# Attention, two MLPs and a gate on one core: the attention's small matmuls in two groups a pair

## The chip, the cores and the metric

The kernel runs on one core of one Trainium2 chip. Its time is the device time of one launch in microseconds, and the time before is the median of three runs. Five engines work beside each other, each with its own queue, which it takes in order: TensorE (PE, matmuls into the accumulator memory PSUM), VectorE (DVE), ScalarE (ACT), GpSimd (POOL) and SyncE (SP, which issues the DMAs). They wait for each other through semaphores.

## The reference

Four batches of 768 tokens go through three stages. All is in float32.

```python
# 1. gated linear attention, 8 heads of 48 channels
for t in range(S):
    state = alpha[:, :, t, :, None] * state + einsum('bhd,bhe->bhde', k[:, :, t], v[:, :, t])
    y[:, :, t] = einsum('bhd,bhde->bhe', q[:, :, t], state)
# 2. x = y as (batch, 768, 384): mixing over tokens by a product of rank 32, then an MLP
h = x.transpose(0, 2, 1) @ U @ V
u = x + h.transpose(0, 2, 1)
x = u + maximum(u @ w_ch1, 0) @ w_ch2          # 384 -> 1536 -> 384
# 3. spatial gating unit
h = maximum(x @ w_in, 0);  u, v = h[..., :512], h[..., 512:]
v_n = (v - mean(v)) / sqrt(var(v) + 1e-6)
out = (u * (einsum('ts,bsd->btd', w_spatial, v_n) + b_spatial[None, :, None])) @ w_out
```

## The kernel before

Two heads make a pair, so there are 4 batches of 4 pairs, numbered 0 to 15. A pair's 768 tokens are cut into 6 chunks of 128. `prepare` (L605) makes running products of alpha over each chunk, backwards (`bw`, a scan on VectorE, L613) and forwards (`fw`, L625), and GpSimd multiplies k by the one and q by the other (L603). Then TensorE has these pieces, all in plain float32, in which one matmul stands as two records in the trace:

- `flip` (L645): five transposes of k; ScalarE copies them out of PSUM (`kn`, L657).
- `scores` (L661): for half the chunks, 6 matmuls k by q. Each uses 64 of TensorE's 128 rows, and the two heads run side by side. VectorE multiplies the result with the causal mask (`mask`, L678: 2 operations for each half).
- `added` (L684): what every chunk adds to the state, 10 matmuls with 64 of 128 columns each, and 2 more that multiply a tile of zeros (`nothing`), so that a scan over the chunks finds zeros where the next row begins. `state` (L697) is that scan on VectorE and two copies by ScalarE.
- `inner` and `outer` (L710, L721): 12 and 10 matmuls, masked scores by v and state by q; each writes 48 columns, the two heads side by side. ScalarE copies the result out in four pieces (`take`, L738).
- For three pairs of a batch there is also the mixing over tokens (`Mix`, L754): two times three transposes (`ps_t`, L763) and a product of 6 matmuls (`ps_g`, L779). These, like `flip`, use the whole array.

The MLP of a batch runs over two blocks of 384 tokens and 12 groups of 128 hidden channels. A group is `up_group` (L313: 9 matmuls in three triples) and, two groups behind, `down_group` (L339: 9 matmuls in three triples, one for each of three accumulators). Its matmuls split float32 into a high and a low part (type fp32r), and have 384 columns. After `up_group` ScalarE makes `h` from the bank (L328), and VectorE makes the remainder `hl` from the same bank (`rest_of_h`, L309), which then is free.

PSUM has 8 banks: 3 for the accumulators (`acc`), 2 for `up_group` (`mm`), and 3 for all of the attention (`x`).

The attention of batch b + 1 is woven into the MLP of batch b. `attend` (L796) is a generator; every `yield` ends a step. `pull` (L1018) is called after nearly every MLP triple and takes the next step when it is due, in equal shares, about one step for every three calls. So the order on each engine is the order in which the program issues: what a step issues stands on every engine behind what the MLP has issued until then and ahead of what comes next. A pair has 8 steps: flip (and the mixing's first transposes); the bw scan of the next pair; scores of the first half (and the second transposes) with their masks; the fw scan; added, scores of the second half, state and masks; a step for moves alone; (the product and) outputs; and loading. Batch 0's attention is `first_batch` (L889) and runs ahead of all this. In the MLP of batch 0 the weights are also loaded and unpacked, piece by piece: ScalarE (L195, L505), VectorE (L196, L199, L207) and GpSimd (L202).

## Time and profile before

| | |
|---|---|
| three runs | 722.79, 723.46, 724.92 us; median 723.46 |
| span of the profiled execution, first to last instruction | 722.5 us |
| PE busy | 699.7 us (97%) |
| PEld (weight loads, beside the matmuls) | 665.8 us (92%) |
| DVE, ACT, POOL busy | 341.0, 267.1, 203.8 us (47%, 37%, 28%) |
| TensorE's mean granted clock | 0.990 of full speed |

The profiled execution's own time is shown as its span alone. By the timeline the MLP of batch 0 runs from about 51 to 139 us, those of batches 1, 2 and 3 take some 87 us each after that, and the gating stage takes the rest, from 400 us on. Attention of batches 1 to 3, which the change touches, lies between 60 and 320 us. A row of the timeline has the start, the time from the first to the last end of the merged instructions, the engine, the line and the shapes. TensorE's instructions overlap: how long one keeps the engine is read from the start of one row to the start of the next.

### The profile page before, as it was taken

To read this page: it belongs to the slowest core of one execution; us is meant where nothing else is said; L and a number is where in the kernel's file an instruction comes from. 1 tells how busy PE (TensorE), PEld (TensorE's weight loads), DVE (VectorE), ACT (ScalarE), POOL (GpSimd) and SP (SyncE) were. 2 spreads that over 40 slices of the span, in tenths; PEclk is the share of its full clock that TensorE was granted. 3 is DMA by queue.
4 is the path that set the end of the run, shared out by engine and by line. 5 is a ranking of instruction groups with operands and counts; after the bars stand their busy time and mean duration, and the time that the engine had idled before them with its cause. 6 is when DMAs were issued, how large, how long until landed. Compare 5 with 4: busy or idle time off the path is not lost.

```text
span 722.5 us, 12138 instructions
## 1 busy us (share of the span) xinstructions
PE 699.7 (97%) x4984; PEld 665.8 (92%) x4984; DVE 341.0 (47%) x585; ACT 267.1 (37%) x542; POOL 203.8 (28%) x171
## 2 busy tenths in 40 slices
PE   7988699999999999999999999999999999999996
PEld 6877599999999999999999999989989989999996
DVE  8877879846444434443332486253152134226211
ACT  3874266643444332444331444232232223224111
POOL 4445434414110122010030043334224123433211
PEclk9999899999999999999999999999999999999998
DMA  9699043330532230500001545120003003000001
GB/s 343 205 341 222 1 80 70 67 68 34 109 73 48 61 59 1 111 5 2 34 1 37 189 131 169 48 73 1 34 1 99 33 1 99 1 33 2 33 34 38
DMA packets 21170, 54.01 MB, mean 75 GB/s; under 512 B 2705, under 2 KB 12817, under 8 KB 19825
## 3 DMA queue, kind: packets, MB, share of 16 engines
q1 hardware_dynamic: 21104, 53.14, 26.6%
q8 instruction: 41, 0.67, 0.4%
q14 instruction: 25, 0.20, 0.1%
HBM read 42.51 MB, written 9.44 MB: 72 GB/s over the span
## 4 chain that ended last, share of the span: by engine, by line
PE 86%; DVE 3%; ACT 1%; POOL 1%; issue 1%; POOLq 0%; ACTq 0%
PE ps L321 20%; PE acc L241 7%; PE acc L242 7%; PE acc L243 7%; PE ps_s L242 5%; PE ps_s L243 5%; PE ps_s L241 4%; PE ps_sc L669 3%; PE ps_y L716 2%; PE ps_o L243 2%; PE ps_o L242 2%; PE ps_o L241 2%; PE ps_v L242 2%; PE ps_v L241 2%; PE ps_v L243 2%; PE ps_u L242 2%
## 5 line engine op out<-in xcount | busy, mean ns | idle before, releaser
L321 PE MATMUL ps<-partuh,w 128*128 128x384 f32 x576 | 135.0, 341 | 7.5 <-ACT w L505 3.3
L321 PEld LDWEIGHTS ps<-partuh,w 128*128 128x128 f32 x576 | 102.8, 190 | 10.7 <-DVE w L207 4.0
L309 DVE SCALAR_TENSOR_TENSOR hl<-ps,h 128x384 fp32r<-128x384 f32 x96 | 53.1, 554 | 120.9 <-ACT h L328 120.1
L241 PE MATMUL acc<-h,w 128*128 128x384 f32 x288 | 99.5, 345 | 0.3 <-DVE ub L354 0.3
L243 PE MATMUL acc<-hl,w 128*128 128x384 f32 x288 | 96.7, 336 | 0.0
L242 PE MATMUL acc<-h,w 128*128 128x384 f32 x288 | 96.6, 335 | 0.0
L328 ACT ACTIVATE h<-ps 128x384 fp32r<-128x384 f32 x96 | 46.9, 488 | 97.3 <-PE ps L321 97.0
L454 DVE TENSOR_TENSOR vsb<-ps_s,bb 128x384 f32<-128x384 f32 x32 | 17.8, 558 | 127.3 <-PE ps_s L243 127.3
L207 POOL TENSOR_TENSOR partul<-ub,partuh 128x384 fp32r<-128x384 f32 x47 | 47.2, 1027 | 102.0 <-ACT partuh L276 89.1
L321 PE MATMUL ps<-partul,w 128*128 128x384 f32 x288 | 68.3, 344 | 1.1 <-POOL partul L207 1.0
L207 POOL TENSOR_TENSOR gl<-gt,gh 128x384 fp32r<-128x384 f32 x32 | 32.4, 1012 | 118.5 <-ACT gh L460 118.5
L242 PE MATMUL ps_s<-wsph,vl 128*128 128x384 f32 x192 | 64.5, 336 | 0.9 <-POOL vl L207 0.9
L241 PE MATMUL ps_s<-wsph,vh 128*128 128x384 f32 x192 | 64.2, 334 | 0.0
L243 PE MATMUL ps_s<-wspl,vh 128*128 128x384 f32 x192 | 64.2, 334 | 0.0
L460 ACT ACTIVATE gh<-gt 128x384 fp32r<-128x384 f32 x32 | 16.8, 526 | 124.5 <-DVE gt L457 124.5
L241 PEld LDWEIGHTS acc<-h,w 128*128 128x128 f32 x288 | 54.3, 189 | 2.9 <-issue 1.2
L242 PEld LDWEIGHTS acc<-h,w 128*128 128x128 f32 x288 | 54.3, 189 | 0.0
L321 PEld LDWEIGHTS ps<-partul,w 128*128 128x128 f32 x288 | 51.5, 191 | 3.0 <-POOL partul L207 1.9
L243 PEld LDWEIGHTS acc<-hl,w 128*128 128x128 f32 x288 | 54.2, 188 | 0.0
L603 POOL TENSOR_TENSOR akq<-akq,bw 128x768 f32<-128x768 f32 (+1 forms) x15 | 24.6, 1638 | 87.8 <-DVE bw L613 85.9
L207 POOL TENSOR_TENSOR vl<-vt,vh 128x512 fp32r<-128x512 f32 x20 | 27.2, 1383 | 50.0 <-ACT vh L424 50.0
L202 POOL TENSOR_TENSOR narrow<-narrow,bits 128x768 uint32<-128x768 uint32 (+2 forms) x14 | 27.7, 1981 | 45.8 <-ACT bits L195 16.0
(154 smaller groups left out, 1369.8 us busy)
## 6 DMA issues: line engine op xcount, KB each, us to landing
akq<-in_akq SPq DMA_DIRECT2D x24, 433.3 KB, 7.2
bits<-in_w SPq DMA_DIRECT2D x12, 768.0 KB, 12.7
x2d<-ub SPq DMA_DIRECT2D x8, 576.0 KB, 3.4
ub<-x2d SPq DMA_DIRECT2D x8, 576.0 KB, 5.2
out_y<-ob SPq DMA_DIRECT2D x24, 192.0 KB, 1.9
v<-in_v SPq DMA_DIRECT2D x15, 288.0 KB, 7.6
words<-in_w_in SPq DMA_DIRECT2D x8, 384.0 KB, 3.3
words<-in_wsT SPq DMA_DIRECT2D x4, 576.0 KB, 6.7
```

The source lines that it names most:

```text
L202: nc.gpsimd.tensor_tensor(out=t, in0=t, in1=low, op=ALU.add)
L207: engine.tensor_tensor(out=out, in0=x, in1=hi.bitcast(F32), op=ALU.subtract)
L241: nc.tensor.matmul(out=ps, lhsT=wh, rhs=xh, start=first, stop=False)
L242: nc.tensor.matmul(out=ps, lhsT=wl, rhs=xh, start=False, stop=False)
L243: nc.tensor.matmul(out=ps, lhsT=wh, rhs=xl, start=False, stop=last)
L309: nc.vector.scalar_tensor_tensor(out=hl, in0=ps[:, 0:TB], scalar=0.0, in1=h.bitcast(F32), op0=ALU.max, op1=ALU.subtract)
L321: nc.tensor.matmul(out=ps[:, 0:TB], lhsT=wx[:, k * 128 : (k + 1) * 128], rhs=ux[:, k, :], start=i == 0, stop=i == len(parts) - 1)
L328: nc.scalar.activation(out=h, in_=ps[:, 0:TB], func=AF.Relu)
L454: nc.vector.tensor_tensor(out=vsb, in0=psv[:, 0:TB], in1=self.g["bb"][:, blk * TB : (blk + 1) * TB], op=ALU.add)
L460: nc.scalar.activation(out=hi, in_=gt, func=AF.Copy)
L603: engine.tensor_tensor(out=chunks(x)[:, c], in0=chunks(x)[:, c], in1=chunks(by)[:, c, 1:CW], op=ALU.mult)
L669: nc.tensor.matmul(out=pts[h][:, j * C : (j + 1) * C], lhsT=self.k[r, c * C : (c + 1) * C], rhs=self.q[r, c * C : (c + 1) * C], start=True ...
```

## The change

For batches 1 to 3 the steps of a pair become: the next pair's bw scan (and the mixing's first transposes); the mixing's second transposes; all twelve scores matmuls, then the MLP's pending `hl`, then four masks; the fw scan; the mixing's product; the flip of the next pair; the outputs, and behind them the next pair's added matmuls and its state; loading. So a pair's state is made one pair earlier, and the first pair of batch 1 gets its flip and its added matmuls in steps of their own ahead of the loop. One of the four score tiles takes a bank of `mm` in place of `x`. The two matmuls with zeros go, and VectorE writes the zeros into PSUM by a MEMSET ahead of the scan. Batch 0's attention stays as it was.

```diff
--- before.py
+++ after.py
@@ -637,10 +637,14 @@
         class Pair:
 
 
-            def __init__(self, n, us, moves, tags):
-                self.n, self.us, self.moves, self.hp, self.tags = n, us, moves, seq[n] % NP, tags
+            def __init__(self, n, tags):
+                self.n, self.hp, self.tags = n, seq[n] % NP, tags
                 self.k, self.q, self.vv, self.decay = ready.pop(n)
                 self.sms, self.pys = [], []
+
+            def bind(self, us, moves):
+                self.us, self.moves = us, moves
+                return self
 
             def flip(self, warm=0):
 
@@ -660,7 +664,7 @@
 
             def scores(self, i, warm=0):
 
-                pts = [ps.tile([128, 512], F32, "ps_sc", self.tags["scores"]) for h in range(2)]
+                pts = [ps.tile([128, 512], F32, "ps_sc", tag) for tag in self.tags["scores"][2 * i : 2 * i + 2]]
                 busy(warm, pts[0])
                 for j in range(CB):
                     c = CB * i + j
@@ -685,7 +689,7 @@
 
                 pd = ps.tile([128, 512], F32, "ps_d", self.tags["state"])
                 busy(warm, pd)
-                for c in range(NC):
+                for c in range(NC if self.n < NP else NC - 1):
                     for h in range(2):
                         if c < NC - 1:
                             k, x = self.kn[:, c, HW * h : HW * (h + 1)], self.vv[:, c, h * D : (h + 1) * D]
@@ -697,6 +701,8 @@
             def state(self, pd):
 
                 after = apool.tile([128, D * NC], F32, name="after", tag="after", bufs=1)
+                if self.n >= NP:
+                    nc.vector.memset(pd[:, NC - 1 : D * NC : NC], 0.0)
                 nc.vector.tensor_tensor_scan(
                     out=after, data0=pd[:, 0 : D * NC], data1=self.decay.rearrange("p e c -> p (e c)"), initial=0.0, op0=ALU.add, op1=ALU.mult,
                 )
@@ -742,15 +748,6 @@
                         for m in range(KE):
                             self.moves.append((self.us[i][HW * h + D : HW * (h + 1), m, :], to[HW * h + 16 * m : HW * h + 16 * (m + 1)]))
 
-            def outputs(self):
-
-                for i in range(NB):
-                    self.inner(i)
-                for i in range(NB):
-                    self.outer(i)
-                for i in range(NB):
-                    self.take(i)
-
         class Mix:
 
 
@@ -793,13 +790,15 @@
                 to, rows = moves.pop(0)
                 nc.sync.dma_start(out=to, in_=rows)
 
+        flying = {}
+
         def attend(b, blocks):
 
-            tags = {"flip": "x", "scores": "x", "state": "x", "out": "x"}
+            tags = {"flip": "x", "scores": ("mm", "x", "x", "x"), "state": "x", "out": "x"}
             us = [up.block() for _ in range(NB)]
             stk = up.pool.tile([3 * R, E], F32R, name="stk", tag="stk")
-            moves, mix, last = [], None, None
-            if b * NP not in ready:
+            moves, mix = [], None
+            if b * NP not in flying:
                 p0 = prepare(b * NP)
                 next(p0)
                 yield
@@ -808,43 +807,51 @@
                 yield
                 yield
                 next(p0)
+                first = flying[b * NP] = Pair(b * NP, tags)
+                first.flip()
+                yield
+                yield
+                first.state(first.added())
                 yield
             for i in range(NP):
                 n = b * NP + i
-                pair = Pair(n, us, moves, tags)
+                pair = flying.pop(n).bind(us, moves)
 
                 ahead = prepare(n + 1)
-                pair.flip()
+                next(ahead, None)
                 if mix:
                     mix.take(mix.flip(0))
                 yield
+                if mix:
+                    mix.take(mix.flip(1))
+                move_some(moves, 3)
+                yield
+                pts = pair.scores(0), pair.scores(1)
+                mlp.rest_of_h()
+                for x in pts:
+                    pair.mask(x)
+                move_some(moves, 3)
+                yield
                 next(ahead, None)
                 yield
-                pts = pair.scores(0)
                 if mix:
-                    pt = mix.flip(1)
-                pair.mask(pts)
-                if mix:
-                    mix.take(pt)
+                    mix.keep(mix.product())
                 move_some(moves, 3)
                 yield
+                if n + 1 < NPAIR:
+                    after = flying[n + 1] = Pair(n + 1, tags)
+                    after.flip()
                 next(ahead, None)
                 move_some(moves, 3)
                 yield
-                pd = pair.added()
-                pts = pair.scores(1)
-                pair.state(pd)
-                pair.mask(pts)
-                next(ahead, None)
-                move_some(moves, 3)
-                yield
-                move_some(moves, 3)
-                yield
-                if mix:
-                    gp = mix.product()
-                pair.outputs()
-                if mix:
-                    mix.keep(gp)
+                for x in range(NB):
+                    pair.inner(x)
+                for x in range(NB):
+                    pair.outer(x)
+                if n + 1 < NPAIR:
+                    after.state(after.added())
+                for x in range(NB):
+                    pair.take(x)
                 yield
                 if n + 3 < NPAIR:
                     load_pair(n + 3)
@@ -891,8 +898,8 @@
             us = [up.block() for _ in range(NB)]
             stk = up.pool.tile([3 * R, E], F32R, name="stk", tag="stk")
             moves, mixes, pairs = [], [], []
-            tags = {"flip": "mm", "scores": "acc", "state": "x", "out": "x"}
-            pair = Pair(0, us, moves, tags)
+            tags = {"flip": "mm", "scores": ("acc",) * 4, "state": "x", "out": "x"}
+            pair = Pair(0, tags).bind(us, moves)
             pair.flip()
             pts = pair.scores(0, 5)
 
@@ -925,7 +932,7 @@
                 later = pair.scores(1)
                 pair.inner(0)
                 next(ahead)
-                after = Pair(n + 1, us, moves, tags)
+                after = Pair(n + 1, tags).bind(us, moves)
                 after.flip(4 if n else 0)
                 pair.mask(later)
                 pair.inner(1)
```

What this makes of the order is shown at three places; lines of the changed kernel's pieces are 4 higher than before (L673 is scores, L698 added, L722 and L731 inner and outer).

TensorE, the first pair of batch 2 (pair 8), before: the second half of its scores stands behind `added` (`ps_d`), between two triples of `up_group` (`ps_1966`).

```order
L321 MATMUL ps_1966<-partuh,w_778 128x384 x3
L694 MATMUL ps_d<-v,kn 64x48 x10
L694 MATMUL ps_d<-ident,nothing 64x48 x2
L669 MATMUL ps_sc<-akq_84 128x128 x6
L321 MATMUL ps_1966<-partul,w_778 128x384 x3
L321 MATMUL ps_1966<-partuh,w_778 128x384 x3
```

The same pair's scores now, all twelve, between the first and the second triple of `up_group` (`ps_1937`):

```order
L321 MATMUL ps_1937<-partuh,w_700 128x384 x3
L673 MATMUL ps_sc<-akq_84 128x128 x12
L321 MATMUL ps_1937<-partul,w_700 128x384 x3
L321 MATMUL ps_1937<-partuh,w_700 128x384 x3
L241 MATMUL acc_1846<-h,w_1588 128x384
```

All twelve now stand where the first six stood before, one group of the MLP earlier than the last six did, and `added` and the matmuls with zeros have left.

TensorE, the outputs of the same pair, before (`ps_y` is written by inner and outer):

```order
L321 MATMUL ps_2022<-partuh,w_833 128x384 x3
L321 MATMUL ps_2022<-partul,w_833 128x384 x3
L716 MATMUL ps_y<-sm,v 48x128 x12
L725 MATMUL ps_y<-akq_84,state_115 48x128 x10
L321 MATMUL ps_2022<-partuh,w_833 128x384 x3
```

The outputs now; `ps_d` here is of pair 9:

```order
L321 MATMUL ps_2027<-partuh,w_833 128x384 x3
L321 MATMUL ps_2027<-partul,w_833 128x384 x3
L722 MATMUL ps_y<-sm,v 48x128 x12
L731 MATMUL ps_y<-akq_84,state_115 48x128 x10
L698 MATMUL ps_d<-v,kn 64x48 x10
L321 MATMUL ps_2027<-partuh,w_833 128x384 x3
```

The next pair's ten `added` matmuls have come in behind outer.

VectorE at the scores of the same pair, before (`hl` is `rest_of_h` of the group whose bank it names, `bw` and `fw` are the scans for pair 9):

```order
L613 SCALAR_TENSOR_TENSOR bw<-akq_85,ends 128x774
L616 RECIPROCAL starts<-bw 128x6
L309 SCALAR_TENSOR_TENSOR hl<-ps_1882,h 128x384
L678 TENSOR_TENSOR sm<-ps_sc,causal 128x384 x2
L625 SCALAR_TENSOR_TENSOR fw<-akq_85,starts 128x774
L309 SCALAR_TENSOR_TENSOR hl<-ps_1925,h 128x384
```

VectorE there now:

```order
L613 SCALAR_TENSOR_TENSOR bw<-akq_85,ends 128x774
L616 RECIPROCAL starts<-bw 128x6
L309 SCALAR_TENSOR_TENSOR hl<-ps_1904,h 128x384
L682 TENSOR_TENSOR sm<-ps_sc,causal 128x384 x4
L625 SCALAR_TENSOR_TENSOR fw<-akq_85,starts 128x774
L309 SCALAR_TENSOR_TENSOR hl<-ps_1937,h 128x384
```

Two more masks now stand ahead of the fw scan and of the `hl` that frees the bank `ps_1937`.

## Rows read from the trace of the kernel before

**Rows 1.** Windows: stretch, length, busy PE, PEld, DVE, ACT, POOL, clock, DMA.
```profile
80.00:87.00 7.00, 5.59 (x25) 4.42 (x24) 4.43 (x6) 2.01 (x4) 2.99 (x2) 0.51 0.00 0
100.00:139.00 39.00, 39.00 (x356) 36.56 (x355) 35.23 (x48) 23.88 (x47) 15.46 (x8) 1.00 0.42 79
...
226.00:313.00 87.00, 87.00 (x701) 83.11 (x699) 35.52 (x59) 32.04 (x69) 16.13 (x12) 1.00 0.29 59
```

**Rows 2.** Timeline of a pair: start, us, engine, line, operation, [idle before].
```profile
282.76 0.68 PE L321 MATMUL ps<-partuh,w 128*128 128x384 f32 x3
283.37 0.94 PE L669 MATMUL ps_sc<-akq 64*128 64x128 f32 x12
...
284.34 1.02 DVE L678 TENSOR_TENSOR sm<-ps_sc,causal 128x384 f32<-128x384 f32 x2 [1.86 <-PE ps_sc L669]
...
284.87 0.70 PE L321 MATMUL ps<-partuh,w 128*128 128x384 f32 x3
285.28 1.76 DVE L625 TENSOR_TENSOR_SCAN fw<-akq,starts 128x774 f32<-128x774 f32 x1
...
285.66 0.49 ACT L328 ACTIVATE h<-ps 128x384 fp32r<-128x384 f32 x1 [3.14 <-PE ps L321]
...
286.95 0.53 DVE L309 SCALAR_TENSOR_TENSOR hl<-ps,h 128x384 fp32r<-128x384 f32 x1
286.98 0.68 PE L321 MATMUL ps<-partuh,w 128*128 128x384 f32 x3
...
287.59 0.79 PE L694 MATMUL ps_d<-v,kn 128*64 128x48 f32 x20
288.21 0.29 PE L694 MATMUL ps_d<-ident,nothing 128*64 128x48 f32 x4
288.43 0.94 PE L669 MATMUL ps_sc<-akq 64*128 64x128 f32 x12
288.80 0.75 DVE L700 TENSOR_TENSOR_SCAN after<-ps_d,decay 128x288 f32<-128x288 f32 x1
...
289.58 1.34 ACT L706 ACTIVATE state<-after 64x240 f32<-64x240 f32 x2 [3.42 <-DVE after L700]
289.92 0.68 PE L321 MATMUL ps<-partuh,w 128*128 128x384 f32 x3
...
292.00 0.68 PE L321 MATMUL ps<-partuh,w 128*128 128x384 f32 x3
...
292.52 0.69 PE L321 MATMUL ps<-partul,w 128*128 128x384 f32 x3
293.14 1.52 PE L716 MATMUL ps_y<-sm,v 128*48 128x128 f32 x24
294.49 1.27 PE L725 MATMUL ps_y<-akq,state 128*48 128x128 f32 x20
295.14 2.01 ACT L738 ACTIVATE y<-ps_y 48x384 f32<-48x384 f32 x4 [2.78 <-PE ps_y L725]
...
296.33 0.34 PE L241 MATMUL acc<-h,w 128*128 128x384 f32 x1
```

**Rows 3.** Timeline: six transposes between the MLP's matmuls.
```profile
155.89 0.82 PE L763 MATMUL ps_t<-ident,ub 128*128 128x128 f32 x6
...
156.73 0.34 PE L242 MATMUL acc<-h,w 128*128 128x384 f32 x1
```

**Rows 4.** Groups by line, VectorE: a MEMSET of few columns.
```profile
L572 DVE MEMSET ends<- 128x6 f32 x1 | 0.1, 63 | 0.1
```

**Rows 5.** Timeline: where TensorE waits in the first batch's MLP.
```profile
73.35 0.79 PE L321 MATMUL ps<-partuh,w 128*128 128x384 f32 x3 [1.79 <-DVE w L207]
...
79.59 0.96 PE L321 MATMUL ps<-partuh,w 128*128 128x384 f32 x3 [3.33 <-ACT w L505]
...
80.44 2.43 DVE L207 TENSOR_TENSOR w<-narrow,w 128x768 fp32r<-128x768 f32 x1
...
82.92 1.33 PE L321 MATMUL ps<-partuh,w 128*128 128x384 f32 x3 [1.41 <-DVE w L207]
```

More of the change, by code (lines that the diff above doesn't have):

```diff
@@ L831, in attend @@
                 next(ahead, None)
+                yield
+                if mix:
+                    mix.keep(mix.product())
                 move_some(moves, 3)
                 yield
-                pd = pair.added()
-                pts = pair.scores(1)
-                pair.state(pd)
-                pair.mask(pts)
+                if n + 1 < NPAIR:
+                    after = flying[n + 1] = Pair(n + 1, tags)
+                    after.flip()
                 next(ahead, None)
@@ L840, in attend @@
                 yield
-                move_some(moves, 3)
-                yield
-                if mix:
-                    gp = mix.product()
-                pair.outputs()
-                if mix:
-                    mix.keep(gp)
+                for x in range(NB):
[6 more added lines that the diff above has]
+                    pair.take(x)
                 yield
```

## The prediction

> **What bounds the kernel now.** I read three views in this order: the windows, to see which engine is full in which stage; the timeline of one pair, for what the attention's pieces cost TensorE; and the timeline where TensorE waits. In the windows the reader is to see that from 226 to 313 us TensorE is busy for all of 87.00 us at full clock, while VectorE has work for 35.52 and ScalarE for 32.04 [rows 1]. There every microsecond that TensorE is spared comes off the time, and nothing else does, unless another engine makes TensorE wait. In the first batch's MLP it is different: from 100 to 139 us TensorE is full too, but VectorE has 35.23 us of work in 39, so only 3.8 us are spare, and from 80 to 87 us TensorE is busy for 5.59 of 7 us at a clock of 0.51, about its lower level of 1.2 GHz [rows 1].
>
> **What the merging saves.** A triple of the MLP takes 0.52 us from start to start (292.00 to 292.52) [rows 2]. So a piece between two triples costs the time from the triple ahead to the one behind it, less 1.04 us for the two. In pair 9 [rows 2]:
> - six scores: 284.87 - 282.76 - 1.04 = 1.07 us;
> - added, zeros and six scores: 289.92 - 286.98 - 1.04 = 1.90 us;
> - outputs: 296.33 - 292.52 - 1.04 = 2.77 us. Together 5.74 us.
>
> Twenty-four records of inner take 1.35 us (293.14 to 294.49), 0.056 each, two halves of the array side by side [rows 2]. Scores have the same 128 columns and also run as two halves, so twelve records should take 0.67 us of their 1.07; 0.40 is the price of going to this kind of matmul and back. Twelve scores in one place then cost 1.07 + 0.67 = 1.74 us. Behind outer, the twenty records of added take what they took, 0.62 us (287.59 to 288.21) [rows 2]: outputs and added cost 2.77 + 0.62 = 3.39. The new sum is 5.13 us, 0.61 less; for 12 pairs 7.3 us. The zeros are in it: 4 records at 0.62 / 20 = 0.031 us, 0.12 a pair.
>
> The joint of outer and added is not in this trace. From above: the step from the zeros to the scores took 0.22 us for 4 records, 0.10 more than the records [rows 2]; 11 such joints are 1.1 us. From below it is nothing, as between inner and outer, which follow each other at one pace. I take nothing, since like inner and outer the two pieces split the columns, while the scores split the rows. The Trainium skill has a rule on this (TensorEngine Tiling (Array Packing), Key Properties): a change of tiling mode, not of the tile, drains TensorE. By that rule the joint is free, as both pieces work in halves of the columns, and the price belongs to the change of mode and not to the group; by the row of the zeros it would be 1.1 us in all.
>
> Transposes and the product now stand in more groups than before. Six transposes between MLP matmuls cost 156.73 - 155.89 - 0.17 = 0.67 us, 0.11 each, with nothing left for entering and leaving [rows 3]. So splitting them costs nothing; flips and products keep their number.
>
> The first pair of batch 1 has added in a group of its own: at most the 0.40 us of a lone scores group more; I take 0.3. Saved on TensorE: 7.0 us; with the open joint 5.9 to 7.0.
>
> The MEMSET writes 48 columns, VectorE's of 6 columns took 63 ns [rows 4], and the remainder with 384 columns read from PSUM 0.53 us [rows 2]; so 0.06 to 0.53, nearer the first, say 0.15. It is on no path while TensorE is full: its cover is the 8 steps until the state is used. Without that cover it would cost 12 times as much, 1.8 us.
>
> **What the change adds.** Scores now hold one of the two `mm` banks. The group that was under way when they came keeps the other, and the next `up_group` needs that one, so it waits for the pending `hl`. Mostly that `hl` was issued ahead of the masks. Where the scores come inside `up_group`, as for the first pairs of batches 2 and 3, it stands behind four masks and the fw scan. Counted from the scores' start: in pair 9 the masks began at 0.97, the fw scan at 1.91 and the `hl` at 3.58 us (283.37 to 286.95) [rows 2]. Two more masks add 0.94, so `hl` ends at 4.52 + 0.53 = 5.05. TensorE asks for the bank after 1.64 us (the 1.74 less what leads in), 1.04 of `up_group` and 1.56 of `down_group`, so at 4.24, perhaps 4.3. It waits 0.8 us, with the signal and the start 0.9; in two places, 1.8 us. Bounds: 0, if VectorE takes the scan later, and 2 x 1.9.
>
> On ScalarE the state copies now stand ahead of the output copies and wait for the scan. In pair 9 the scan starts 0.37 us after TensorE has gone on (288.43 to 288.80) and takes 0.75; with 0.15 for the MEMSET, 1.34 for the state copies, 2.01 for the outputs, 0.49 for the next `h` and 0.53 for its `hl` [rows 2] the bank is free about 5.6 us after the MLP has resumed. Where the outputs come ahead of the last triple of `up_group`, its bank is asked for again after that triple, two `down_group` and one `up_group`, 0.6 + 3 x 1.56 = 5.3 us. I put 0.2 us on each of the four times that this is close (two pairs, and the scores behind them), 0.8 in all; bounds 0 and 3.
>
> The queues behind: POOL waits for the same scans, now a step earlier for bw, and is idle beside them. SP's moves of pair 3 of the batch start a step earlier, and its loads stay at the end of the pair; no wait for a DMA ends last here.
>
> **The first batch.** TensorE waits 1.79 us (until 73.35, for VectorE's low weights), 3.33 (until 79.59, for ScalarE's high ones) and 1.41 (until 82.92, for low ones) [rows 5]. The weights set these ends, so TensorE's work that the change puts ahead of them is free: the flip of pair 4 (5 x 0.11) goes ahead of the first, added (0.62 and its 0.3) ahead of the second. In the third, VectorE's step took 2.43 us from 80.44 [rows 5], behind the bw scan of pair 5; that scan now comes after it, and the state's scan, which is shorter, before. I count 0.5 + 0.9 + 1.0 = 2.4 us gained. Against it: after the first outputs `h` waits behind 3.35 us of ScalarE's copies, VectorE's queue stands behind its `hl`, and then come weights and the bw scan of 1.8 us ahead of the next `hl`; I count 0.6 + 1.6 = 2.2 us of new waits. So nothing remains, between -3 and +3. From 80 to 87 us the clock is low, after TensorE had stood for 3.33 us [rows 1, 5]. Added now breaks that pause in two. If the clock stays up, half of 5.59 us, 2.8, is won too; I think it more likely that it falls again, since in sum the pause is nearly as long.
>
> **Sum.** -7.0 + 1.8 + 0.8 + 0 = -4.4 us. The profiled span is 722.5 us, so 718.1; the median of the runs is 0.96 above that span, which I keep: 719.1 us.
>
> **Rivals.**
> 1. No wait comes, or the clock stays up: then the 7.0 us stand whole, and of what the first batch may add (0 to 2.8) I take the middle, 1.5: 723.5 - 7.0 - 1.5 = 715.0 us. For it: outside the first batch no engine but TensorE is over half busy [rows 1]. Against: the order on VectorE is fixed, and two of the waits follow from it.
> 2. The gain turns into a wait in every pair. Price: the bank that the scores hold is missed each time, by 0.6 us, 12 x 0.6 = 7.2; the time stays at about 723.7. The Trainium skill names the sign (Perfetto Trace Analysis, Optimization Strategy): the same gap again and again on the engine that should be full can mean that there are too few PSUM buffers. For it: `mm` has but two banks. Against: in 9 of 12 pairs the order has the needed `hl` ahead of the masks.
> 3. Slower: in the first batch ScalarE's queue holds VectorE up. At each of four outputs (pairs 4 to 7) `h` stands behind state and output copies, 1.34 + 2.01 us [rows 2], and VectorE, which needs it for `hl`, stands as long: 4 x 3.35 = 13.4 us, of which 3.8 are spare [rows 1]. 9.6 + 2.6 - 7.0 = 5.2 us slower, 728.7. It decides from 3.8 + 4.4 + 2.2 = 10.4 us of standing, 2.6 at each output. For it: VectorE is at 90% there. Against: such a stand counts only where the scan or weights behind it are late, and weights have some groups of slack.
> 4. The merging doesn't do what it says, and the 0.40 us belongs to each six scores and not to the change of kind: only zeros go, 1.4 us, less the waits: 724.5. Against: full-array pieces show no such price [rows 3].
>
> **Chances.** Forecast (717.0 to 721.3) 0.45; rival 1 0.2; rival 2 0.2; rival 3 0.1; rival 4 0.05. A measurement of this kernel tells 0.3% (2.2 us) from no change. Faster by more: the forecast and rival 1, 0.65. Within: rival 2 and rival 4, 0.22 with a part of their spread given to the slower side. Slower: rival 3 and that part, 0.13. The range of 8 in 10 goes from 714.8 to 723.7; it leaves out rival 3, part of rival 4 and a little of rival 1.
>
> **What would show it.** Right: in the windows of the MLPs of batches 1 and 2 TensorE stays full or nearly so, scores cost 1.74 us and outputs with added 3.39, and TensorE's waits show two of about 0.9 us on VectorE's `hl`, at the `up_group` after the first scores of batches 2 and 3. Wrong: a wait of `up_group` on `hl` in most pairs (rival 2), VectorE idle behind `h` between 90 and 139 us with TensorE waiting (rival 3), a scores group of 2.1 us (rival 4), or added behind outer well over 0.62 us.

## The result, and the profile after

The changed kernel takes 734.03 us in the median (733.71 to 734.66, 4 runs), beside 723.37 (722.79 to 724.92) for the kernel before: ratio 1.014, 95% interval 1.0127 to 1.0153. It is 10.7 us slower, where 719.1 was forecast in a range of 714.8 to 723.7. The profiled span is 732.0 us.

Windows of the changed kernel, with the columns of [rows 1]:

```profile
80.00:87.00 7.00, 7.00 (x48) 6.50 (x46) 4.82 (x8) 3.18 (x6) 3.51 (x2) 0.76 0.00 0
100.00:139.00 39.00, 32.99 (x267) 30.02 (x268) 28.88 (x42) 19.01 (x38) 16.87 (x8) 0.95 0.29 54
139.00:226.00 87.00, 81.93 (x687) 77.54 (x684) 41.41 (x69) 37.34 (x79) 21.45 (x14) 0.98 0.35 72
226.00:313.00 87.00, 86.44 (x691) 83.13 (x690) 34.75 (x60) 30.57 (x66) 14.44 (x11) 1.00 0.26 54
313.00:400.00 87.00, 85.69 (x674) 82.35 (x674) 30.97 (x60) 29.63 (x64) 12.74 (x10) 1.00 0.05 13
```

From 100 to 139 us, where TensorE had been full at full clock [rows 1], it is now busy for 32.99 us of 39, and from 139 to 226 us for 81.93 of 87. In the later stretches a little is missing too, 0.56 and 1.31 us. VectorE, of which I had written that it had 3.8 us to spare, works *less* between 100 and 139 us (28.88 us): it stands.

So the loss can be read from where the MLPs begin. The first triple of the MLPs of batches 1, 2 and 3 in the changed kernel:

```profile
182.44 0.68 PE L321 MATMUL ps<-partuh,w 128*128 128x384 f32 x3
...
290.62 0.68 PE L321 MATMUL ps<-partuh,w 128*128 128x384 f32 x3
...
396.40 0.68 PE L321 MATMUL ps<-partuh,w 128*128 128x384 f32 x3
```

The same triples in the kernel before:

```profile
171.98 0.68 PE L321 MATMUL ps<-partuh,w 128*128 128x384 f32 x3
...
279.06 0.69 PE L321 MATMUL ps<-partuh,w 128*128 128x384 f32 x3
...
386.19 0.68 PE L321 MATMUL ps<-partuh,w 128*128 128x384 f32 x3
```

The MLP of batch 0 with what is woven into it thus ends 10.46 us later; that of batch 1 adds 1.1 and that of batch 2 takes 1.35 off again; behind it the lag stays as it is until the gate. (Batch 0's MLP now also holds flip and added of the next batch's first pair, 0.55 + 0.62 us, which batch 2's MLP gives back.)

These starts correct what stands above on the kernel before. Its MLP of batch 0 runs to 171.98 us and not to 139, those of batches 1 and 2 take 107 us each and not 87, and the gating stage begins near 465 us and not at 400. The window from 139 to 226 us thus holds the end of batch 0's MLP and the first half of batch 1's. And the pair of [rows 2], called pair 9, is pair 12, the first of batch 3; its costs stand as they were read.

The pieces themselves cost what they should. Outputs of pair 8 with added of pair 9, and scores of pair 12, in the timeline of the changed kernel:

```profile
194.88 0.68 PE L321 MATMUL ps<-partul,w 128*128 128x384 f32 x3
...
197.94 0.74 PE L698 MATMUL ps_d<-v,kn 128*64 128x48 f32 x20
...
198.61 0.79 PE L321 MATMUL ps<-partuh,w 128*128 128x384 f32 x3
198.83 0.10 DVE L705 MEMSET ps_d<- 128x48 f32 x1 [5.26 <-PE ps_d L698]
...
199.24 0.33 PE L241 MATMUL acc<-h,w 128*128 128x384 f32 x1
...
293.74 0.69 PE L321 MATMUL ps<-partuh,w 128*128 128x384 f32 x3
...
294.35 1.61 PE L673 MATMUL ps_sc<-akq 64*128 64x128 f32 x24
...
296.52 0.68 PE L321 MATMUL ps<-partuh,w 128*128 128x384 f32 x3
...
298.60 0.68 PE L321 MATMUL ps<-partuh,w 128*128 128x384 f32 x3
298.87 0.53 DVE L309 SCALAR_TENSOR_TENSOR hl<-ps,h 128x384 fp32r<-128x384 f32 x1
```

Read as in the prediction, twelve scores cost 296.52 - 293.74 - 1.04 = 1.74 us and outputs with added 199.24 - 194.88 - 1.04 = 3.32 (forecast 1.74 and 3.39). The MEMSET takes 0.10 us and follows added at once. What was removed and added on TensorE was priced right; the loss is waiting. (The last two lines, the start of the next `up_group` and the `hl` of the group before it, are taken up with the bank of `mm` below.)

### The profile page after: what moved, and what is told of

Read it like the earlier page. It is cut to its first block, busy times and chain, and to the rows that moved or that the text cites. A ratio compares the mean times of both kernels' runs of the same rounds, so it can differ in the third digit from the quotient of the medians.

```text
span 732.0 us, 12040 instructions
## 1 busy us (share of the span) xinstructions
PE 699.6 (96%) x4936; PEld 666.6 (91%) x4936; DVE 337.8 (46%) x597; ACT 266.0 (36%) x542; POOL 207.0 (28%) x171
## 4 chain that ended last, share of the span: by engine, by line
PE 73%; DVE 7%; ACT 7%; POOL 3%; issue 2%; POOLq 0%; DVEq 0%; ACTq 0%
PE ps L321 15%; PE acc L241 5%; PE acc L243 5%; PE acc L242 5%; PE ps_s L242 5%; PE ps_s L243 4%; PE ps_s L241 4%; PE ps_y L722 2%; PE ps_o L241 2%; PE ps_o L243 2%; PE ps_o L242 2%; PE ps_v L242 2%; PE ps_v L241 2%; PE ps_v L243 2%; PE ps_u L242 2%
## 5 line engine op out<-in xcount | busy, mean ns | idle before, releaser
L241 PE MATMUL acc<-h,w 128*128 128x384 f32 x288 | 100.9, 350 | 1.4 <-DVE ub L354 1.4
L242 PE MATMUL acc<-h,w 128*128 128x384 f32 x288 | 97.3, 338 | 0.0
L202 POOL TENSOR_TENSOR narrow<-narrow,bits 128x768 uint32<-128x768 uint32 (+2 forms) x14 | 29.5, 2106 | 58.6 <-DVE narrow L199 25.6
L603 POOL TENSOR_TENSOR akq<-akq,fw 128x768 f32<-128x768 f32 (+1 forms) x15 | 26.4, 1759 | 58.3 <-DVE fw L625 53.6
```

The source lines that it names most:

```text
L202: nc.gpsimd.tensor_tensor(out=t, in0=t, in1=low, op=ALU.add)
L241: nc.tensor.matmul(out=ps, lhsT=wh, rhs=xh, start=first, stop=False)
L242: nc.tensor.matmul(out=ps, lhsT=wl, rhs=xh, start=False, stop=False)
L603: engine.tensor_tensor(out=chunks(x)[:, c], in0=chunks(x)[:, c], in1=chunks(by)[:, c, 1:CW], op=ALU.mult)
```

## Where TensorE waits now

The five longest waits of TensorE between 85 and 175 us (us in total, times, longest); the kernel before has none there:

```profile
PE ps L321 <- DVE hl L309: 2.4, 1, 2.4
PE ps_sc L673 <- ACT yb L767: 1.8, 2, 1.3
PE ps_y L722 <- ACT kn L661: 1.7, 1, 1.7
PE ps_t L760 <- ACT ub L744: 1.7, 3, 0.7
PE acc L241 <- DVE ub L354: 1.1, 1, 1.1
```

After the two longest single waits the clock is at its lower level, 1.2 GHz, for some 3 us (windows of the changed kernel):

```profile
108.00:111.00 3.00, 3.00 (x11) 3.00 (x10) 3.00 (x5) 1.18 (x2) 0.64 (x1) 0.50 0.07 16
139.00:142.00 3.00, 3.00 (x32) 2.89 (x30) 0.78 (x1) 1.02 (x2) 0.00 (x0) 0.50 0.02 5
```

3 us at half speed are at least 1.5 us lost each time, on top of the pause.

How such a wait is made can be followed through one chain: ScalarE, VectorE and TensorE of the changed kernel from the outputs of pair 4 on:

```profile
97.74 1.33 ACT L712 ACTIVATE state<-after 64x240 f32<-64x240 f32 x2 [0.40 <-DVE after L706]
...
99.10 2.02 ACT L744 ACTIVATE y<-ps_y 48x384 f32<-48x384 f32 x4
...
101.14 0.49 ACT L328 ACTIVATE h<-ps 128x384 fp32r<-128x384 f32 x1
...
101.66 0.56 DVE L309 SCALAR_TENSOR_TENSOR hl<-ps,h 128x384 fp32r<-128x384 f32 x1 [3.10 <-ACT h L328]
...
103.59 1.76 DVE L613 TENSOR_TENSOR_SCAN bw<-akq,ends 128x774 f32<-128x774 f32 x1
...
105.39 0.62 ACT L619 ACTIVATE decay<-bw 128x240 f32<-128x240 f32 x1 [2.83 <-DVE bw L613]
...
106.02 0.47 ACT L328 ACTIVATE h<-ps 128x384 fp32r<-128x384 f32 x1
106.52 0.56 DVE L309 SCALAR_TENSOR_TENSOR hl<-ps,h 128x384 fp32r<-128x384 f32 x1 [0.93 <-ACT h L328]
...
107.13 0.44 PE L321 MATMUL ps<-partuh,w 128*128 128x384 f32 x1 [2.44 <-DVE hl L309]
```

The state copies wait for the scan; the output copies stand behind them, `h` behind those, and VectorE stands 3.10 us for `h`. Behind two steps of a weight comes the next pair's bw scan (1.76 us), ahead of the next `hl`. ScalarE meanwhile has the copy of the decays at the head of its queue, which needs that scan (2.83 us of standing), and the next `h` is behind it. So two queues hold each other up in turn, and `up_group` gets its bank 2.44 us late, ten microseconds after the MLP had gone on at 96.58. (The other bank of `mm` holds scores of pair 5 from 102.36 us until their masks, which are issued behind that `hl`.) With the states of pair 9 the chain is the same link for link:

```profile
199.75 1.30 ACT L712 ACTIVATE state<-after 64x240 f32<-64x240 f32 x2 [4.27 <-DVE after L706]
...
201.07 2.02 ACT L744 ACTIVATE y<-ps_y 48x384 f32<-48x384 f32 x4
...
203.11 0.49 ACT L328 ACTIVATE h<-ps 128x384 fp32r<-128x384 f32 x1
...
203.64 0.56 DVE L309 SCALAR_TENSOR_TENSOR hl<-ps,h 128x384 fp32r<-128x384 f32 x1 [3.92 <-ACT h L328]
...
204.11 1.76 DVE L613 TENSOR_TENSOR_SCAN bw<-akq,ends 128x774 f32<-128x774 f32 x1
...
205.91 0.63 ACT L619 ACTIVATE decay<-bw 128x240 f32<-128x240 f32 x1 [2.30 <-DVE bw L613]
...
206.55 0.85 ACT L328 ACTIVATE h<-ps 128x384 fp32r<-128x384 f32 x2
207.05 1.02 DVE L309 SCALAR_TENSOR_TENSOR hl<-ps,h 128x384 fp32r<-128x384 f32 x2 [0.95 <-ACT h L328]
...
207.75 0.49 PE L673 MATMUL ps_sc<-akq 64*128 64x128 f32 x4 [1.12 <-POOL akq L603]
```

The profile names GpSimd's multiplication of k as the releaser of the scores of pair 9; that k belongs to the pair after. The first of the two `hl` (the first 0.55 of 1.02 us from 207.05) ends just ahead of 207.75 too, and it is the one that frees the bank of `mm` that the scores take.

## Experiments

In the table the lag is the start of batch 1's MLP less its start in the kernel before; the next two columns are what the MLPs of batches 1 and 2 then add. By the prediction's terms, without any wait, they would be -1.0 (-2.45 saved, 1.17 made ahead, 0.3 for the lone added), -2.45 and -3.6.

```
kernel                         median   ratio to before, 95%       lag   batch 1  batch 2
the change                     734.03   1.0140 (1.0127-1.0153)   +10.46   +1.09   -1.35
states a step later            720.38   0.9943 (0.9927-0.9960)    +2.96   -2.23   -3.66
outputs copied first           724.42   1.0003 (0.9993-1.0012)    +6.01   -2.25   -3.66
bw scan a step later           735.31   1.0153 (1.0136-1.0170)   +14.92   -0.93   -2.61
scores apart                   735.29   1.0153 (1.0136-1.0170)    +8.26   +2.48   +0.41
zeros only (on before)         723.27   0.9985 (0.9975-0.9994)    +1.18   -0.45   -0.45
states later, flip earlier     719.97   0.9934 (0.9919-0.9950)    +2.54   -2.30   -3.72
states later, batch 1 apart    722.53   0.9973 (0.9959-0.9987)    +2.20   -2.23   -3.66
states later, batch 1 as before 719.71  0.9935 (0.9919-0.9950)    +0.14   -0.99   -3.66
outputs copied later           728.44   1.0067 (1.0044-1.0090)    +7.38   -0.34   -2.63
states later, scores apart     726.41   1.0037 (1.0024-1.0050)    +2.35   +0.51   -0.68
states later, flip earlier, pace 718.14 0.9918 (0.9899-0.9938)    +0.73   -2.54   -3.72
pace only                      731.50   1.0110 (1.0093-1.0127)    +7.85   +0.89   -1.37
```

Each lag is read from one execution. The kernel before itself lies between 722.8 and 725.8 us over its runs, and zeros only, which by its terms takes 0.5 us from the first batch, shows +1.18: the clock is low (0.50) from 79.1 to 89.2 us there, and in the kernel before from 80.2 to 86.8. So parts of the first batch's lag below some 2 us are not told from chance by a lag alone.

**1. States a step later.** In the step of the outputs:

```diff
-                    after.state(after.added())
+                    pd = after.added()
                 for x in range(NB):
                     pair.take(x)
                 yield
+                if n + 1 < NPAIR:
+                    after.state(pd)
```

> The scan and the two copies of the next pair's states are issued one step later, behind the output copies and a stretch of the MLP. Theory Q (queues: after the merged outputs h stands behind 1.34 us of state copies and 2.01 us of output copies on ScalarE, hl behind h, and the bw scan between one hl and the next): h no longer waits for VectorE's scan and the state copies, 1.3 to 2 us at each of 12 places. TensorE's wait of 2.44 us at 107.13 us (with the 1.7 us that the low clock costs behind it) and the two of 1.1 us at the scores of pairs 9 and 13 go or halve: 727 to 730 us. Theory M (the mm bank lent to the scores makes TensorE need an hl that is behind the masks, wherever the state copies stand): the waits on hl stay, 733 to 735 us.

It takes 720.38 us: some 14 less than the change, well beyond what was expected, and faster than before. Here `h` comes 0.93 us after TensorE has gone on (192.04, the MLP's next triple at 191.11), where it came 4.50 later (203.11 and 198.61):

```profile
190.00 2.02 ACT L744 ACTIVATE y<-ps_y 48x384 f32<-48x384 f32 x4 [2.02 <-PE ps_y L731]
...
191.11 0.79 PE L321 MATMUL ps<-partuh,w 128*128 128x384 f32 x3
...
192.04 0.49 ACT L328 ACTIVATE h<-ps 128x384 fp32r<-128x384 f32 x1
...
194.05 1.32 ACT L712 ACTIVATE state<-after 64x240 f32<-64x240 f32 x2 [1.52 <-DVE after L706]
...
198.59 1.61 PE L673 MATMUL ps_sc<-akq 64*128 64x128 f32 x24
```

Scores now start with no wait, and batches 1 and 2 save 2.23 and 3.66 us, the prediction's 2.45 and 3.6 all but whole. What is left is in the first batch (waits of TensorE, 85 to 400 us):

```profile
PE acc L241 <- DVE ub L354: 2.6, 1, 2.6
PE ps_y L722 <- ACT kn L661: 1.6, 1, 1.6
PE ps L321 <- DVE hl L309: 1.0, 1, 1.0
```

**2. Outputs copied first.** The same step, with the state behind the four copies instead of a step later:

```diff
-                    after.state(after.added())
+                    pd = after.added()
                 for x in range(NB):
                     pair.take(x)
+                if n + 1 < NPAIR:
+                    after.state(pd)
                 yield
```

> In the step of the outputs the four output copies stand ahead of the scan's state copies on ScalarE; h still comes behind all six. Theory Q: only ScalarE's wait for MEMSET and scan goes (0.37 + 0.10 + 0.75 = 1.2 us at each place, since the output copies can run meanwhile), so h comes 1.2 us earlier and not 3.3: about half the effect of moving the states a step, 729 to 732 us. Theory M: 733 to 735 us.

724.42 us, more than the half expected. `h` still stands behind all six copies, but the output copies fill the time in which ScalarE waited for the scan, and `h` comes 2.49 us after TensorE goes on (196.63, after 194.14). In batches 1 and 2 that is as good as a step later; in the first batch 3.05 us of lag remain between the two.

**3. The bw scan a step later.**

```diff
                 ahead = prepare(n + 1)
-                next(ahead, None)
                 if mix:
                     mix.take(mix.flip(0))
                 yield
+                next(ahead, None)
```

> The bw scan of the next pair (1.76 us) with its decay copy goes from step 1 to step 2, so it no longer stands right behind the late hl after the outputs. Theory Q: the hl at 106.52 us comes 1.8 us earlier and TensorE's wait of 2.44 us falls to about 0.7, the clock stays up there (1.7 us), and the scores of pairs 9 and 13 no longer wait 1.1 us for hl: 727 to 730 us. Theory M: the scan is not what the bank waits for, 733 to 735 us. Should the scan now meet the scores' hl instead, the wait moves by one step and the time stays.

The sum says no effect, and the stretches say why that is no answer: batches 1 and 2 gain 2.0 and 1.3 us, and the waits of scores of 1.1 us are gone, so the scan (with its decay copy, which moves along) is a link of the chain there. The first batch loses 4.5 more, in longer waits for `ub` (3.4 us) and `yb` (4.2 us). This expectation failed in the first batch.

**4. Scores apart.**

```diff
-                pts = pair.scores(0), pair.scores(1)
-                mlp.rest_of_h()
-                for x in pts:
-                    pair.mask(x)
+                pair.mask(pair.scores(0))
                 move_some(moves, 3)
                 yield
+                pair.mask(pair.scores(1))
                 next(ahead, None)
                 yield
```

(and all four tiles from `x`.)

> Scores go back to two groups of six in two steps, all from the x banks; outputs and added stay merged, bw and the states stay where the change put them. On TensorE this costs the second entry again, 12 x 0.40 = 4.8 us. Theory M: all waits that come from the lent bank go, at least 2 x 1.1 at the scores and the up_group's 2.44 with its 1.7 of clock: 734.0 + 4.8 - 6.3 = 732.5 us or less, with no wait of TensorE for hl. Theory Q: hl is late because h is, the up_group at 107 us waits as before, only the two of 1.1 us go: 734.0 + 4.8 - 2.2 = 736.6 us.

About 1 us slower than the change, between the two theories. No wait for `hl` over 0.2 us is left in batches 1 and 2, but they lose 1.4 and 1.75 us: the second entries cost 4 x 0.40 = 1.6 in each, and `acc` now waits 0.96 us for `ub` once in each. So some 1 us a batch was won without the lent bank, and lending it was not what mattered most. In the first batch scores wait for a mask instead (2.7 us), which stands behind the same late `h` and bw scan.

**5. Zeros only**, on the kernel before:

```diff
-                for c in range(NC):
+                for c in range(NC if self.n < NP else NC - 1):
...
+                if self.n >= NP:
+                    nc.vector.memset(pd[:, NC - 1 : D * NC : NC], 0.0)
```

> The kernel before, with one edit: the four matmuls that wrote zeros in each pair of batches 1 to 3 are a MEMSET on VectorE (48 columns of 64 x 2 rows). By the prediction's working 4 x 0.031 = 0.12 us a pair, 1.5 us for 12 pairs, and the MEMSET is hidden: ratio 0.998. A rival: the MEMSET holds the state's scan and the masks behind it up, so nothing or a loss remains: 1.000 or more.

Ratio 0.9985, 0.4 to 1.8 us saved; the MLPs of batches 1 and 2 gain 0.45 us each, where 4 x 0.12 = 0.48 was worked out.

**6. Flip a step earlier**, on experiment 1:

```diff
                     mix.keep(mix.product())
-                move_some(moves, 3)
-                yield
                 if n + 1 < NPAIR:
                     after = flying[n + 1] = Pair(n + 1, tags)
                     after.flip()
+                move_some(moves, 3)
+                yield
                 next(ahead, None)
```

> On the kernel with the states a step later: the next pair's flip goes from step 6 to step 5, behind the product. What is left of the first batch's loss by the trace are three waits: 1.0 us for hl at 105.6, 2.6 us for VectorE's sum ub at 113.8 with 1.7 us of low clock behind it, 1.6 us at 137.7 where the merged outputs need x banks that hold the flip until ScalarE's kn copies, which stand behind a weight copy. Theory Q: the last of the three goes, since kn has a step more: 720.4 - 1.6 = 718.8 us. Rival: kn meets the same weight copy a step earlier, or the flip's banks now hold the product or the scores up: 720.4 or more.

The wait for `kn` is gone, but another of 1.1 us came at 146.5 us, and the gain is 0.4 us, not 1.6; the runs of the two kernels overlap (719.36 to 720.26 and 720.14 to 720.87 us).

**7. Batch 1 alone with scores apart**, on experiment 1:

```diff
-                pts = pair.scores(0), pair.scores(1)
+                if b == 1:
+                    pair.mask(pair.scores(0))
+                    move_some(moves, 3)
+                    yield
+                    pair.mask(pair.scores(1))
+                else:
+                    pts = pair.scores(0), pair.scores(1)
...
```

> On the kernel with the states a step later: batch 1 alone (whose attention lies in the first batch's MLP) has its scores in two groups of six in two steps, from x banks; batches 2 and 3 keep twelve in one place. Costs 4 x 0.40 = 1.6 us on TensorE. Theory Q: four masks in one go (1.9 us), a weight step (0.9) and the fw scan (1.8) are what makes hl and ub late at 105 to 114 us; with the masks in two goes these waits (1.0 + 2.6 + 1.7 of clock) go by half or more, so 718.5 to 720 us. Rival: VectorE has too little room there in any order (35 us of work in 39 before), the waits only move: 720.4 + 1.6 = 722 us.

Inconclusive. Its executions lie between 719.57 and 723.67 us, with mean clocks from 0.995 to 0.988; the profiled one is the fastest. There scores wait 1.4 us and `acc` for `ub` 2.9, about as much as without the edit: the waits moved, as the rival said.

**8. Batch 1 as before**, on experiment 1: batch 1 runs the loop of the kernel before, batches 2 and 3 the new one.

```diff
-        more = attend(1, nxt)
+        more = attend_apart(1, nxt)
```

> On the kernel with the states a step later: batch 1 (in the first batch's MLP) goes back to the order of the kernel before, with only its zeros by MEMSET; batches 2 and 3 keep the merged groups. By the terms of the prediction batches 2 and 3 save 2 x 2.45 = 4.9 us, less 0.3 for the lone added, and the zeros of batch 1 0.5: 724.3 - 5.1 = 719.2 us if the first batch runs as before. If the loss of the first batch does not come from batch 1's order but from what the two first pairs of the program or the weights do, the time stays at 722 or more.

719.71 us, 0.5 from the forecast of its terms. The first batch runs as before (+0.14), and the two others save what the terms say: batch 1's MLP, -2.45 + 1.17 + 0.3 = -0.98, measured -0.99. The loss of the first batch comes from the new order there.

**9. Outputs copied later**, the mirror of experiment 1.

```diff
                 if n + 1 < NPAIR:
                     after.state(after.added())
+                yield
                 for x in range(NB):
                     pair.take(x)
-                yield
```

> The mirror of the first experiment: in the changed kernel the state's scan and copies stay in the step of the outputs, and the four output copies go a step later. So h again stands behind two copies fewer time (2.01 us less), but the x banks that hold the outputs are given back a step later instead of earlier. Theory Qh (what costs is h, and through hl the bank of the next up_group, standing behind the copies): like the first experiment, 721 to 727 us. Theory Qx (what costs is the x banks, which the outputs hold until ScalarE has copied them, so that the next pair's transposes and scores wait): the transposes' and scores' waits on ScalarE's copies grow, 732 to 738 us.

728.44 us: neither theory alone. `h` now comes 2.48 us after TensorE goes on (197.99, after 195.51), as in experiment 2, and one wait of 0.2 us for `hl` is left behind 175 us. But the mixing's transposes wait for the output copies (waits of TensorE, 175 to 400 us):

```profile
PE ps_t L760 <- ACT ub L744: 1.4, 3, 0.5
```

Not for their banks alone, as theory Qx has it: the transposes read the very `ub` that these copies write (`Mix.flip` and `take` in the kernel). In the change, too, those of pair 9 begin at 222.97 us, 0.06 behind the second output copy, while the scan has left the bank of `ps_d` at 220.54. Whether a bank was ever short for them, no run separates.

Experiments 2 and 9 have `h` equally late and differ in when the outputs are copied: the copies end 0.90 and 4.87 us after TensorE goes on. Between them lie 1.9 and 1.0 us in batches 1 and 2; between 9 and the change, which copies the outputs about as late (4.48) but makes `h` later, 1.4 and 1.3. So the 5.6 us there are about half late outputs and half late `h`.

**10. States later and scores apart:** the edits of experiments 1 and 4 together.

```diff
-            tags = {"flip": "x", "scores": ("mm", "x", "x", "x"), "state": "x", "out": "x"}
+            tags = {"flip": "x", "scores": ("x",) * 4, "state": "x", "out": "x"}
```

> On the kernel with the states a step later: scores go back to two groups of six in all three batches, from x banks alone, so no mm bank is lent. By the prediction's term a second entry into this kind of matmul costs 0.40 us: 12 x 0.40 = 4.8 us, of which 8 x 0.40 = 3.2 in batches 2 and 3, where no wait is left that the lent bank could have caused. Term right: the stretch of batches 2 and 3 is 3.2 us longer than with the states a step later, the whole 723 to 725 us. If the 0.40 belongs to the scores themselves and not to the entry: 720.4. If the lent bank still costs something: under 720.

Batches 1 and 2 lose 2.7 and 3.0 us against experiment 1. Two waits for `ub` of 0.96 us are in it; the other 3.8 us over 8 pairs are 0.47 a pair, where 0.40 was the price of a second entry. So that price belongs to entering this kind of matmul, and the rival by which it belongs to the scores falls. The medians differ by 6.0 us, where 2.6 to 4.6 was expected.

**11. Pace**, on experiment 6, and **12. pace only**, on the change:

```diff
-                n_steps, late = N_STEPS + 4, 12
+                n_steps, late = N_STEPS + 8, 12
```

> On the kernel with states later and flip earlier: the steps of batch 1 are spread over the first batch's MLP as if there were four more of them, so each comes earlier (the change put three steps ahead of batch 1's first pair and left the number by which they are spread). If part of the first batch's loss is that its steps end late and close together: 717 to 719 us. If VectorE's share of weights sets it: 720 or more, since the steps then meet the weights earlier.

718.14 us, faster than both kernels: ratio 0.9918 to the one before.

> The changed kernel, with the steps of batch 1 spread as if there were four more (as in the run before), and nothing else: states, output copies and flip stay where the change put them. If the pace was a cause of its own in the first batch, it gives here what it gave with the states moved, 1.8 us: 732 us. If the late steps only matter where ScalarE's copies already hold h up, more: 728 to 731. If they meet the weights earlier and the copies still stand ahead of h: 734 or more. Batches 2 and 3 keep their waits in each case (5.8 us).

731.50 us, by the ratios some 2 less than the change. The change puts two more steps ahead of batch 1's first pair, and the number by which the steps are spread stayed. So attention's pieces come later among the MLP's matmuls: from 88 to 105 us the MLP stands some 3 to 6 us further than before. So the pace counts by itself, by the lags 1.8 and 2.6 us, in the first batch alone. The edit adds four to the number, two more than the steps that came in, so it also sets an earlier pace than before; what two would give, and what the kernel before would take with four, no run shows.

## Why the prediction was wrong

**The saving** (5.13 us a pair in place of 5.74, 7.0 in all) was right, by the pieces' rows and by batches 1 and 2 of experiments 1 and 8. The joint of outer and added, taken as free, is free: 3.32 us. The Trainium skill (TensorEngine Tiling (Array Packing), Key Properties) has it that the array drains at a change of the tiling mode and not of the tile; the 0.47 us for a second entry into scores and the free joint agree.

**The bank of `mm`** (1.8 us, at pairs 8 and 12) failed in its place, and not by its times. Behind the scores at 294.35 the next `up_group` asks for its bank after 4.25 us (298.60) and the `hl` begins after 4.52 (298.87), just as worked out. But TensorE starts at 298.60 without waiting for it (at pair 8 at 190.66, ahead of the `hl` at 190.90): of the two banks the group ahead holds one until that `hl`, so the `up_group` has the one that the scores gave back with their masks. The step that failed is "the next `up_group` needs that one". The waits for a bank of `mm` stood at the scores of pairs 9 and 13 instead.

**ScalarE's backlog** (0.8 us, bounds 0 to 3) is the first term that was mis-sized: 5.8 us in batches 1 and 2 (1.09 + 2.45 and -1.35 + 3.6), of which experiment 1 gives 5.6 back. I had counted from the resumption to a free bank once, 5.6 us against 5.3, and had put 0.2 us on the difference, at four places. The chain does not stop at that bank: the bw scan that the change puts right behind it on VectorE, and the decay copy ahead of the next `h` on ScalarE, pass the delay on to the second `hl`, which is where it shows (1.12 us at 207.75). The Trainium skill (PSUM — Partial Sum Buffer, Engine vs sequencer instructions) calls the queues of ScalarE and VectorE strictly first in, first out, and the chain bears it out at every link. That the mixing's transposes wait for the output copies, which now come later, I had not counted at all.

**The first batch** ("nothing remains, between -3 and +3") is the step that failed most. Its early gains came: TensorE's waits of 1.79, 3.33 and 1.41 us [rows 5] became 1.18, 0.63 and 2.47, in sum 2.3 us less where 2.4 was counted, and the low clock got shorter (0.76 from 80 to 87 us, 0.51 before [rows 1]). But the new waits, put at 2.2 us, were over five times that: the lag is +10.46 where the terms give -1.0, so 11.4 us were lost, with these gains already taken off. By the experiments, taken in this order, 4.45 us of it are the output copies behind the state copies (2), 3.05 more `h` behind the state copies (1), 0.4 the flip's place (6, within chance) and 1.8 the pace (11); 1.7 us are left, in which one wait of 2.19 us at 102.63 us stands, with a low clock behind it.

**Rival 3** was the right mechanism, with a chance of 0.1: ScalarE's copies ahead of `h`, VectorE standing behind it. Its price for the first batch, 13.4 - 3.8 = 9.6 us, is near the 11.4 measured, though not all of those are such stands (the pace is in them); its 2.6 us for the other two batches fall short of the 5.8, and its 728.7 of the 734.0. I gave it little because "such a stand counts only where the scan or weights behind it are late", and they were: a stand of 3 us with 3.8 us to spare in 39 uses up most of the slack at once. It also went on in batches 1 and 2, where I had argued that no engine but TensorE is over half busy, and in the first batch behind 139 us, where VectorE before had work for 18.73 us of 33. Averages hid it: from the end of added (198.68) to the second `hl`, VectorE's gaps are waits for ScalarE (3.92 and 0.95 us) and ScalarE's are waits for VectorE (the last 1.07 of its 4.27, and 2.30).

**Rival 2** (the bank missed in every pair) is wrong in its form: behind the first batch two of eight pairs lost 1.1 us at the scores.

**Where the 5.8 us of batches 1 and 2 lie** the idle times alone do not tell: they come to some 3.5 us. Set beside experiment 1, matmul by matmul, the change falls behind at these places: 3.3 us at the `up_group` and the scores of pairs 9 and 13, 1.6 at the mixing's transposes behind the outputs, and 0.6 inside the scores of pair 11, which wait for banks that two `yb` copies give back and take 2.16 us in place of 1.61:

```profile
248.40 2.16 PE L673 MATMUL ps_sc<-akq 64*128 64x128 f32 x24
```

A pause costs more than its idle time: transposes with 0.05 to 0.25 us of idle time ahead of them come 0.3 to 0.4 us later.

**Open** is the first batch's end. No run took away its last 1.7 us, so that its one wait is their cause is argued and not shown, and its smaller parts are read from single executions.

## What to carry to other kernels

When a change puts copies, scans or waits ahead of the instruction that frees the full engine's bank, follow the delay around the loop of queues until it dies out, and not only to the first bank: each engine that takes its queue in order hands it on, whatever its average load. When a merged step is long, issue what is needed soonest first (here the output copies, then `h`), and what is needed a whole pair later in a step of its own. And when steps are added to a woven schedule, count what the pace is worked out from again.

## What the runs showed of the hardware

VectorE's weight step takes 0.93 us alone and 2.44 when it starts behind a multiplication of GpSimd; [rows 5] had shown such a one of 2.43, and I had not asked why. From the timelines of the change and then of experiment 11:

```profile
97.62 0.93 DVE L207 TENSOR_TENSOR w<-narrow,w 128x768 fp32r<-128x768 f32 x1
```
```profile
99.51 1.69 POOL L603 TENSOR_TENSOR akq<-akq,bw 128x768 f32<-128x768 f32 x1 [4.00 <-DVE bw L613]
99.58 2.44 DVE L207 TENSOR_TENSOR w<-narrow,w 128x768 fp32r<-128x768 f32 x1
...
102.63 2.20 PE L673 MATMUL ps_sc<-akq 64*128 64x128 f32 x23 [2.19 <-DVE hl L309]
```

It ends 0.82 us after GpSimd does (102.02 and 101.20), as if it had stood until then; the one of [rows 5] ends 0.81 after its multiplication (82.86 and 82.05). The Trainium skill (SBUF — State Buffer, SBUF: two separate sides) has GpSimd and some VectorE operations lock a shared pair of ports, so that the one that starts second is blocked until the first is done; these rows agree. Four of the weight steps between 85 and 140 us took 2.2 to 2.4 us in experiment 11, each begun 0.06 to 0.29 us behind such a multiplication and ended 0.81 us behind its end; in two that began within 0.01 us of one the step took 0.92, and the multiplication 2.47 in place of 1.69. `hl` stands behind the step at 99.58, and the scores wait 2.19 us for it: the last long wait of the fastest version. A MEMSET of 48 strided columns in PSUM took 0.10 us, so of the bounds of 0.06 to 0.53 the lower was the nearer.
